# A fused linear-attention and gated-MLP kernel: one ordering rule between a ScalarE Exp and a TensorE sum, and a new hand-written order of all 1160 steps

## The chip, the cores and the metric

One core of one Trainium2 chip. The time is device microseconds of one execution of the whole kernel; the median of three runs is given, with the lowest and the highest.

## What is computed

The first half is a recurrent attention with a decay `alpha`, the second a gated MLP that mixes along the sequence. Batch 4, 8 heads, 768 steps, 48 columns per head, so rows of 8 x 48 = 384; the MLP has 1024 columns, half for `u` and half for `v`.

```
state = 0
for t in range(S):
    state = alpha[t][:, None] * state + outer(k[t], v[t])
    y[t] = q[t] @ state
x = y, heads side by side
h = relu(x @ w_in);  u, v = h[:, :512], h[:, 512:]
v_n = (v - mean(v)) / sqrt(var(v) + 1e-6)
v_s = w_spatial @ v_n + b_spatial        # along the sequence
out = (u * v_s) @ w_out
```

## The kernel before

The recurrence runs in chunks of 128 steps, 24 in all (i = 0 to 23), six to a batch. Chunks 0 to 7 are done two at a time, in pairs j = 0 to 3 (`pair`); chunks 8 to 23 one by one (`first`). The steps have short names, and the order is a list of these names:

- `ac kc qc vc`: loads of alpha, k, q and v (L436 for a pair, L646 for a chunk), all issued by SyncE's queue (SP).
- `lnp` takes the logarithm of alpha (ScalarE, L447). `cump j 0` and `cump j 1` (TensorE, L456) sum it along the steps, for the even and the odd rows, each into a bank of PSUM. `totp j` (TensorE, L473, 8 small matmuls) puts the totals of the pair into spare columns of the bank of the odd rows.
- `einvp j par` (ScalarE, L464) is the inverse Exp, exp(-x), of such a bank into `binvp`; `eexpp j par` (ScalarE, L485) is the forward Exp, in place in the bank. `ebcp j` (L559) is the Exp of the totals. `par` 0 is the first of the two, 1 the second.
- `ktp` and `qtp` (L490, L497) multiply k and q by these; `tr` (L518) transposes them; `ev` copies the transposes out of PSUM; `vbp` casts v.
- `updq` (L553) makes the pair's state updates, `z i` (L333, L335, VectorE) adds one to the state, `S i` (L340, VectorE or GpSimd) multiplies by the decay, `sb i` (L200, GpSimd, two casts) writes the state where TensorE reads it. These go from chunk to chunk, one after the other.
- `sc` (L583) makes the scores, `m` (L594) masks them, `ya` (L610) and `y i` (L623) make the output of a chunk from the scores and from the state of the chunk before.
- `xs`, `xt` and `xe` cast the output (L198 or L200), transpose it (L370 for pairs, L393 for single chunks) and copy it into `xT`.
- For single chunks the same steps are `cum` (L666, L669), `einv`, `eexp`, `trk` (L719), `upd` (L740), `sc` (L754), `y` (L776, L782).
- The MLP, for batch b: `v b c` and `u b f h` (three matmuls each with `w_in`, L828), `bn`, `rs`, `vn` (the normalization: L893/L894, L917/L918, then L925 on VectorE or L931 and L934 on GpSimd), `s` (six matmuls with the transposed spatial weights, in two halves, L828), `g` (L989), `o` (four matmuls with `w_out`, L828) and `st`, the store (L1046).

Every engine runs its own instructions in the order in which `replay` emits them. That order is `PLAN`, a table of 1160 words: a letter for the engine (P TensorE, D VectorE, A ScalarE, G GpSimd, S and Q a DMA's issue and its landing) and the number of the step. Numbers behind a P, as in `P119:448:128`, are columns of filler matmuls (`junk`, L188) that TensorE runs ahead of the step. Many steps may stand on one of two engines, and the table says which. The table comes from a search that is not part of the file; `replay` only asserts that each step stands behind the steps that it names in `got(...)`.

TensorE's matmuls differ in the part of the array that they use. L583 uses 48 rows by 64 columns, L553, L610, L393, L719 and L840 64 by 128, L754 48 by 128, L857 1 by 128; all others use 128 by 128.

Of the kernel before, what the change touches and what calls it, by code (L numbers as in the profile page):

```python
# [58 lines left out]
P119:448:128:64:192:192:384 P68 G63 S114 Q115 P58 A70 P69 P129 A59 S112 Q113 G72 P130 A80 A60 D61 A71 G74 A120 S180
Q181 D73 A121 P64:512 D6 A141 A131 P75:128 D62 A132 P77:128 S116 Q117 D123 A78 P66:128 D134 A76 P79 A67 D65 S184 Q185  # L60
G122 D81 P90 D82 P265 D84 A266 D92 G85 S182 Q183 A188 P87:64:192 D91 G133 P127 P125 A128 D88 P199 G8 P200 P138 A201
D89 P136 S19 Q20 G83 A202 A211 P189:192 D135 A139 G124 D126 A190 S186 Q187 G10 P140 A191 P93 D204 A137 D7 D142 P97 A94
S325 Q326 D143 P148 A98 D193 P95 G203 P208 D145 A96 P197 D149 P99 P151 G192 A100 D150 A198 P206 S24 Q25 A209 D153 A207
P195:64:64 A23 P267 G21 D22 P218 A196 G144 A268 D152 P101 D219 S329 Q330 G146 P104 A102 D220 A205 G194 P215 S327 Q328
P154 A105 D217 G86 P210 D216 G147 A333 P155 P159 D212 P221 D213 A156 D103 S29 Q30 P222 A160 G214 P344 S331 Q332 P157
P334 A346 D223 G27 P161 A158 P226 D106 P345 A162 G26 P163 A335 A347 D227 P174 A356 A164 D28 D349 P224 A336 S33 Q34
P168 D165 A225 S386 Q387 P228 P230 A229 D338 A175 G348 P233 A169 D176 A231 P353 G337 P342 S390 Q391 P351 A354 D232
P172 A107 P170 A234 G32 D343 P340 A352 D173 P166 A177 G31 D171 A341 P366 A167 D235 G108 P250 S37 Q38 P247 A350 A252
P243:64 S388 Q389 G178 D367 A248 A249 P239 A251 D368 G339 A35 S428 Q429 P241 G36 D240 P355 A394 D244 P253 G109 A236
D179 P395 P245 A254 S430 Q431 G237 A255 D357 A242 D358 P273 D238 A396 G359 P277 D360 A397 A246 D361 P274 A399 G362  # L70
P278 D400 D275 P256 S392 Q393 G40 P363 A258 A257 P281 D364 A39 P282 S41 Q42 G398 D279 P269 D365 S432 Q433 G280 P259
P262 D283 P402 A260 A263 P270 D264 G276 A261 D404 A403 P293 A436 D271 G284 P294 S499 Q500 P409 D295 P369 G401 D410
P373 P437 G272 D374 P405 A439 P297 A370 S465 Q466 D411 A438 P375 P371 P298 D376 S467 Q468 G440 A372 A441 P412 D299 A45
P377 S434 Q435 G296 A413 D442 P285 D406 A378 G44 P414 P444 A46 D379 G407 A416 P380 G408 S503 Q504 P286 D415 D446 A381
P420 D43 S501 Q502 D445 A473 P426 D287 A507 P301 D382 S471 Q472 A421 G288 A427 P451 P508 G443 S469 Q470 D453 P417 A509
G300 D452 A511 P447 S596 Q597 P474 A302 P424 D448 A475 D512 P309 S505 Q506 G510 A418 A425 P422 D419 A476 G480 A478
S598 Q599 P454 A310 G477 P289 A455 S630 Q631 D479 P290 A383 D449 P481 A423 D291 S600 Q601 P456 G450 P514 A457 D483
# [1096 lines left out]
```

## Time and profile before

| | |
|---|---|
| median of 3 runs | 141.24 us (140.65 to 141.47) |
| the profiled execution | 141.2 us, of which 139.4 us is the span from the first to the last instruction |
| busy, share of the span | TensorE 95%, VectorE 86%, GpSimd 71%, ScalarE 70% |
| granted TensorE clock | 0.996 |
| moved by DMA | 28.64 MB, mean 205 GB/s |

How to read it: a group of instructions shows the line, the engine, the operation, what it writes and reads, the shapes and the count, then the busy time, the mean duration in ns, and the idle time of the engine just before with what ended it. PE is TensorE's matmul, PEld its weight load, which runs beside matmuls; DVE is VectorE, ACT ScalarE, POOL GpSimd, SP SyncE. Matmuls overlap, so that TensorE's real pace is read from the start of one to the start of the next, and a busy PE may still be waiting a little. In the timeline the columns are the start, the time taken and the instructions; behind them, in brackets, the idle time ahead and its releaser.

### The profile page before, as it was taken

How to read it: one execution, taken by the hardware profiler on the slowest of the kernel's cores; microseconds unless marked ns; L12 is line 12 of the kernel's file. 1: busy time of each engine (PE TensorE's matmuls, PEld its weight loads, DVE VectorE, ACT ScalarE, POOL GpSimd, SP SyncE). 2: the span in 40 equal slices, each digit the busy share in tenths (PEclk: the TensorE clock that was granted, in tenths of full speed). 3: DMA queues.
4: the chain of work that ended last, by engine and by line, in shares of the span. 5: the costliest groups of instructions: out<-in, count | busy, mean ns of one | idle time of the engine just before them, and what ended most of it. 6: DMA issues, size and time to landing. Idle time of an engine off the chain costs nothing.

```text
span 139.4 us, 5013 instructions
## 1 busy us (share of the span) xinstructions
PE 133.0 (95%) x1931; PEld 85.0 (61%) x1931; DVE 120.3 (86%) x283; ACT 97.9 (70%) x278; POOL 99.1 (71%) x176
## 2 busy tenths in 40 slices
PE   6999789999999999999999999999999999999990
PEld 4677566756666656665666765655566665555660
DVE  7159899999998898888999999999798999987970
ACT  3597768899944979999975798898772776840011
POOL 6964996697899868697098899988779574382300
PEclk9999999999999999999999999999999999999998
DMA  4999999999989999799999989999981040007635
GB/s 108 324 323 325 289 326 334 312 240 319 282 190 281 182 217 218 151 232 173 197 211 190 232 165 197 203 214 259 291 164 42 0 163 16 0 3 286 224 143 196
DMA packets 89000, 28.64 MB, mean 205 GB/s; under 512 B 83728, under 2 KB 87440, under 8 KB 88976
## 3 DMA queue, kind: packets, MB, share of 16 engines
q1 hardware_dynamic: 88944, 28.32, 82.0%
q8 instruction: 15, 0.25, 0.7%
q14 instruction: 9, 0.07, 0.1%
q0 software_dynamic: 32, 0.00, 0.0%
HBM read 23.60 MB, written 4.72 MB: 203 GB/s over the span
## 4 chain that ended last, share of the span: by engine, by line
PE 78%; POOL 7%; SPq 4%; DMA 4%; DVE 2%; issue 2%; ACT 1%; ACTq 0%; POOLq 0%; DVEq 0%
PE bank L828 54%; SPq L436 4%; DMA kc<-in_k_dram 4%; PE bank L754 3%; PE bank L719 3%; POOL vn L934 2%; PE bank L782 2%; PE bank L740 2%; PE bank L666 2%; PE bank L776 2%; PE bank L393 1%; PE bank L518 1%; POOL sbd L200 1%; POOL kt L490 1%; PE bank L583 1%
## 5 line engine op out<-in xcount | busy, mean ns | idle before, releaser
L828 PE MATMUL bank<-w_spT,vn 128*128 128x384 bf16 x192 | 36.2, 326 | 0.1
L989 POOL TENSOR_TENSOR gT<-vsb,uT 128x384 bf16<-128x384 f32 x24 | 22.0, 928 | 5.6 <-DVE vsb L976 5.3
L828 PEld LDWEIGHTS <-vn 128*128 128x128 bf16 x192 | 17.3, 97 | 12.1 <-POOL vn L934 1.3
L765 DVE TENSOR_TENSOR ptm<-bank,mask 128x512 bf16<-128x512 f32 x32 | 20.6, 682 | 1.2 <-PE bank L754 1.0
L828 PE MATMUL bank<-xT,w_in 128*128 128x384 bf16 x96 | 19.7, 326 | 0.0
L976 DVE TENSOR_TENSOR vsb<-bank,bsp_bc 128x384 f32<-128x384 f32 x31 | 16.8, 553 | 3.1 <-PE bank L828 2.2
L828 PE MATMUL bank<-w_out_sb,gT 128*128 128x384 bf16 (+1 forms) x100 | 18.7, 319 | 0.0
L828 PE MATMUL bank<-w_in,xT 128*128 128x512 bf16 x72 | 18.7, 379 | 0.0
L690 POOL TENSOR_TENSOR kt<-kc,binv 128x384 bf16<-128x384 f32 x15 | 13.6, 913 | 6.5 <-ACT binv L678 6.3
L200 POOL CAST sbd<-state 64x192 bf16<-64x192 f32 x40 | 14.1, 352 | 5.5 <-DVE state L340 2.4
L934 POOL TENSOR_SCALAR vn<-v_sb,rstd,nb 128x512 bf16<-128x512 bf16 x17 | 13.6, 799 | 1.7
L893 DVE BATCH_NORM_STATS2 stats<-v_sb 128x6 f32<-128x512 bf16 x20 | 13.6, 681 | 0.8 <-ACT v_sb L208 0.8
L208 ACT ACTIVATE v_sb<-bank 128x512 bf16<-128x512 f32 x18 | 10.8, 599 | 3.6 <-PE bank L828 3.6
L208 ACT ACTIVATE uT<-bank 128x384 bf16<-128x384 f32 x18 | 8.8, 494 | 5.6 <-PE bank L828 5.5
L828 PEld LDWEIGHTS <-gT 128*128 128x128 bf16 x100 | 8.9, 97 | 5.4 <-DVE gT L989 0.2
L198 ACT COPY kqT<-bank 128x256 f32<-128x256 f32 x32 | 11.1, 381 | 1.1 <-PE bank L719 1.1
L828 PEld LDWEIGHTS <-w_in 128*128 128x128 bf16 x96 | 8.4, 98 | 5.2 <-DVE w_in L200 0.3
L188 PE MATMUL bank<-junk 128*128 128x64 f32 (+5 forms) x32 | 9.7, 433 | 1.1 <-DVE junk L1059 1.1
L594 DVE TENSOR_TENSOR ptm<-bank,mask 128x512 bf16<-128x512 f32 x16 | 10.1, 680 | 0.4 <-PE bank L583 0.2
L198 ACT CAST x_sb<-bank 128x384 bf16<-128x384 f32 x19 | 8.8, 481 | 2.1 <-PE bank L782 1.4
L700 DVE TENSOR_TENSOR qt<-qc,bank 128x384 bf16<-128x384 f32 x16 | 8.7, 549 | 1.1 <-ACT bank L695 1.0
L828 PEld LDWEIGHTS <-xT 128*128 128x128 bf16 x72 | 6.0, 97 | 5.1 <-ACT xT L198 0.2
(133 smaller groups left out, 297.8 us busy)
## 6 DMA issues: line engine op xcount, KB each, us to landing
ac<-in_alpha_dram SPq DMA_DIRECT2D x16, 192.0 KB, 3.9
qc<-in_q_dram SPq DMA_DIRECT2D x16, 192.0 KB, 3.8
kc<-in_k_dram SPq DMA_DIRECT2D x16, 192.0 KB, 3.9
vc<-in_v_dram SPq DMA_DIRECT2D x16, 192.0 KB, 3.8
raw_w<-in_moe_w_spatial_dram SPq DMA_DIRECT2D x3, 768.0 KB, 6.8
out_dram<-raw_w SPq DMA_DIRECT2D x11, 192.0 KB, 3.3
out_dram<-o_sb SPq DMA_DIRECT2D x9, 192.0 KB, 2.3
ac<-in_alpha_dram SPq DMA_DIRECT2D x4, 384.0 KB, 4.4
```

What stands on the lines that cost most here:

```text
L188: nc.tensor.matmul(out=flat[:, 0:cols].rearrange("p (a b) -> p a b", a=4), lhsT=junk, rhs=junk[:, None, 0:n].to_broadcast([128, 4, n]), st ...
L198: nc.scalar.copy(out=out, in_=in_)
L200: ENG[eng].tensor_copy(out=out, in_=in_)
L208: nc.scalar.activation(out=out, in_=in_, func=AF.Relu)
L594: nc.vector.tensor_tensor(out=st[f"ptm{par}"][:, s], in0=st[f"pt{s}{par}"], in1=mask2[:, par], op=ALU.mult)
L690: ENG[eng].tensor_mul(out=k_blocks(kt3)[:, :, :, 0:D], in0=quad(st["kc"]), in1=st["binv"])
L765: nc.vector.tensor_tensor(out=st["ptm"][:, s], in0=st[f"pt{s}"], in1=mask4, op=ALU.mult)
L828: return lambda ps: nc.tensor.matmul(out=out(ps), lhsT=lhsT(), rhs=rhs(), start=start, stop=stop)
L893: nc.vector.bn_stats(out=stats, in_=d["v_sb"][:, tt, :])
L934: nc.gpsimd.tensor_scalar(out=d["vn"][:, t, :], in0=d["v_sb"][:, t, :], scalar1=d["rstd"][:, t:t + 1], scalar2=nb, op0=ALU.mult, op1=ALU.add)
L976: nc.vector.tensor_tensor(out=hold["vs"], in0=ps[:, 0:TH], in1=bsp_bc[:, th, :], op=ALU.add)
L989: ENG[eng].tensor_tensor(out=bt[b]["gT"][:, dsl, cols], in0=hold["vs"], in1=bt[b]["uT"][:, dsl, cols], op=ALU.mult)
```

## The change

Three things. `totp j` is recorded behind `einvp j 1` and depends on it, where it depended on `cump j 1` alone. `eexpp j 1` depends on `totp j` as well as on `einvp j 1`. And the whole table is another one. Lines behind the edit move down by two (L828 becomes L830, and so on) and L485 becomes L486. No step is added or taken away, and no instruction's shape changes.

```
-                op(("totp", j), "PE", 0.2, tot, got(("cump", j, 1), ("c_half",)), prio=P + 2.5, use=[sl_c[1]])
-
             op(("einvp", j, par), "ACT", 0.38, einv, got(("cump", j, par), ("ktp", *divmod(2 * j + par - 3, 2))), prio=P + 3,
                use=[sl_c[par]])
 
+            if par == 1:
+                op(("totp", j), "PE", 0.2, tot, got(("einvp", j, 1), ("c_half",)), prio=P + 2.5, use=[sl_c[1]])
+
...
-            op(("eexpp", j, par), "ACT", 0.38, eexp, got(("einvp", j, par)), prio=P + 3.1, use=[sl_c[par]])
+            op(("eexpp", j, par), "ACT", 0.38, eexp,
+               got(("einvp", j, par), *((("totp", j),) if par else ())), prio=P + 3.1, use=[sl_c[par]])
```

The first line of the table, before and after:

```
-S110 Q111 D0 D15 D2 G16 D5 S49 Q50 D3 D4 D1 D13 G9 D11 S55 Q56 G47 Q48 D12 D17 G14 A118 S51 Q52 G18 A57 S53 Q54
+S110 Q111 D0 D17 D5 G47 Q48 D3 D6 D1 S49 Q50 D11 D2 D15 S53 Q54 D13 D12 G14 D4 A118 S51 Q52 G16 A57 S55 Q56
```

It also hands steps to other engines. Over the whole program VectorE has 15 of the 24 `vn` instead of 7, 3 of the 20 `S` instead of 10, and 7 of the 32 `u` copies instead of 14; GpSimd has 17 `S` instead of 10 and 9 `vn` instead of 17; ScalarE has 25 `u` copies instead of 18.

ScalarE at the start, before: the Exps of pairs 0 and 1 (`binvp` is the inverse, a bank onto itself the forward Exp, `bc` the Exp of the totals).

```order
L464 ACTIVATE binvp_114<-bank_86 128x384
L464 ACTIVATE binvp_113<-bank_87 128x384
L559 ACTIVATE bc_223<-bank_86 128x8
L485 ACTIVATE bank_87<-bank_87 128x384
L485 ACTIVATE bank_86<-bank_86 128x384
L464 ACTIVATE binvp_115<-bank_85 128x384
L485 ACTIVATE bank_85<-bank_85 128x384
L559 ACTIVATE bc_240<-bank_88 128x8
```

The same place now:

```order
L464 ACTIVATE binvp_113<-bank_86 128x384
L486 ACTIVATE bank_86<-bank_86 128x384
L464 ACTIVATE binvp_114<-bank_87 128x384
L464 ACTIVATE binvp_115<-bank_85 128x384
L486 ACTIVATE bank_87<-bank_87 128x384
L464 ACTIVATE binvp_113<-bank_88 128x384
L486 ACTIVATE bank_85<-bank_85 128x384
L561 ACTIVATE bc_246<-bank_87 128x8
```

The even rows of pair 0 (now bank 86) come first with both of their Exps, and between the two Exps of the odd rows (bank 87) stands an Exp of pair 1; the Exp of the totals moved from third to eighth.

GpSimd at the start, before: from pair 0's k product to the state of chunk 3 (`state<-state,bc` is `S`, `sbd<-state` is `sb`, `mask_118` is half of a pair's mask, `mask_96` the mask of single chunks).

```order
L490 TENSOR_TENSOR kt_111<-kc,binvp_114 128x4x2x48
L200 CAST vbp<-vc 128x384
L490 TENSOR_TENSOR kt_112<-kc,binvp_115 128x4x2x48
L340 TENSOR_TENSOR state<-state,bc_223 128x192
L490 TENSOR_TENSOR kt_112<-kc,binvp_113 128x4x2x48
L253 MEMSET ut_ones 128x128
L246 AFFINE_SELECT ut_ones<-ut_ones 128x128
L200 CAST sbd_119<-state 64x4x48 x2
L200 CAST vbp<-vc 128x384
```

The same place now:

```order
L492 TENSOR_TENSOR kt_111<-kc,binvp_114 128x4x2x48
L340 TENSOR_TENSOR state<-state,bc_246 128x192
L246 AFFINE_SELECT mask_118<-mask_118 64x512 x2
L492 TENSOR_TENSOR kt_112<-kc,binvp_113 128x4x2x48
L200 CAST vbp<-vc 128x384
L340 TENSOR_TENSOR state<-state,bc_246 128x192
L200 CAST sbd_119<-state 64x4x48 x2
L492 TENSOR_TENSOR kt_111<-kc,binvp_115 128x4x2x48
L492 TENSOR_TENSOR kt_111<-kc,binvp_114 128x4x2x48
L340 TENSOR_TENSOR state<-state,bc_301 128x192
```

All five `S` of chunks 0 to 4 stand on GpSimd now, where two did, and half a mask that stood ahead of the k product stands behind the first `S`; one k product of pair 1 went to VectorE.

TensorE in the middle of the third batch, before: the end of the transpose of chunk 18's output (L393) and what follows.

```order
L393 MATMUL bank_89<-ident,x_sb 128x64
L393 LDWEIGHTS x_sb
L393 MATMUL bank_85<-ident,x_sb 128x64
L828 LDWEIGHTS vn
L828 MATMUL bank_86<-w_spT,vn 128x384
L828 LDWEIGHTS vn
L828 MATMUL bank_86<-w_spT,vn 128x384
```

The same transpose now:

```order
L393 MATMUL bank_90<-ident,x_sb 128x64
L393 LDWEIGHTS x_sb
L393 MATMUL bank_85<-ident,x_sb 128x64
L721 LDWEIGHTS kt_112
L721 MATMUL bank_86<-ident,kt_112 128x64
L721 LDWEIGHTS kt_112
L721 MATMUL bank_87<-ident,kt_112 128x64
```

Behind the transpose, which uses 64 rows of the array, stood a matmul with all 128 rows; now the transposes of two chunks' k and q follow (L721), which use 64 rows as well.

More of the change, by code (lines that the diff above doesn't have):

```diff
@@ L57 @@
 PLAN = """
-S110 Q111 D0 D15 D2 G16 D5 S49 Q50 D3 D4 D1 D13 G9 D11 S55 Q56 G47 Q48 D12 D17 G14 A118 S51 Q52 G18 A57 S53 Q54
[L59 to L77, printed above, removed]
@@ new lines @@
+S598 Q599 G510 A310 D448 P454 A302 S600 Q601 A425 P422 D512 G288 A383 D455 P481 A423 P514 G449 D482 P456 A483 P305
+D457 G292 A515 D419 A516 P484 A458 S602 Q603 A306 P488 D485 P517 A604 D490 P459 G486 S667 Q668 A513 D519 G450 P605
+A460 P313 S669 Q670 D489 G487 A606 P317 D518 A607 A609 G608 S630 Q631 A314 P491 D461 P520 A492 S709 Q710 G611 P321
+D610 A521 G384 D318 P493 S632 Q633 P612 A495 D494 P522 A462 P615 D613 P496 D523 A614 D524 G464 A675 D322 P532 A497
+P525 S634 Q635 D533 A498 D385 P619 A526 D616 S713 Q714 P534 D463 A527 P536 D621 S671 Q672 A638 P538 D528 A717 P548
@@ L109 @@
+P1129 S323 Q324 D1127 G1120 S578 Q579 P1130 P1132 D1131 G1128 P1140 A1133 P1152 S1134 Q1135 D1141 P1144 A1153 S1142
+Q1143 P1136 A1145 S1154 Q1155 P1148 S1146 Q1147 D1137 P1156 S1138 Q1139 A1149 A1157 S1150 Q1151 S1158 Q1159
 """
```

74 lines of the change are left out of this document (43 added, 31 removed).

## The prediction

> **What bounds the kernel now.** I read the page first, then the busy times by stage, then the timeline of TensorE and of the three engines that feed it.
>
> ```profile
> PE 133.0 (95%) x1931; PEld 85.0 (61%) x1931; DVE 120.3 (86%) x283; ACT 97.9 (70%) x278; POOL 99.1 (71%) x176
> PE   6999789999999999999999999999999999999990
> PEclk9999999999999999999999999999999999999998
> ```
>
> TensorE is busy in every slice but the first and the last few, and at full clock in 39 of 40 slices. By stage (the columns are the stretch, its length, then the busy time of each engine; the borders are where the first single chunk begins and where the last chunk's output is transposed):
>
> ```profile
> 0.00:36.30 36.30, 33.31 (x580) 23.30 (x580) 29.71 (x77) 28.16 (x73) 27.55 (x57) 1.00 1.01 293
> 36.30:118.00 81.70, 81.56 (x1242) 51.16 (x1238) 74.99 (x173) 63.42 (x188) 65.32 (x110) 1.00 0.86 184
> 118.00:139.40 21.40, 18.09 (x120) 10.57 (x116) 15.56 (x35) 6.36 (x18) 6.27 (x10) 0.98 0.38 139
> ```
>
> In the middle TensorE has 81.56 of 81.70 us, VectorE 6.7 us left, the others more. So a gain in the middle can only come from TensorE's own order, and a loss from an engine that makes it wait. Busy does not say that it streams at its pace; for that I read starts in TensorE's timeline:
>
> ```profile
> 32.40 0.65 PE L828 MATMUL bank<-xT,w_in 128*128 128x384 bf16 x3
> 32.98 0.42 PE L583 MATMUL bank<-kqT 48*64 48x128 bf16 x16
> ...
> 90.43 0.65 PE L828 MATMUL bank<-xT,w_in 128*128 128x384 bf16 x3
> 91.01 0.40 PE L754 MATMUL bank<-kqT 48*128 48x128 bf16 x8
> ...
> 92.08 0.65 PE L828 MATMUL bank<-xT,w_in 128*128 128x384 bf16 x3
> 92.57 0.81 PE L828 MATMUL bank<-w_in,xT 128*128 128x512 bf16 x3
> 93.22 0.65 PE L828 MATMUL bank<-xT,w_in 128*128 128x384 bf16 x3
> ...
> 117.78 0.48 PE L393 MATMUL bank<-ident,x_sb 64*128 64x64 bf16 x12
> 118.19 0.66 PE L828 MATMUL bank<-xT,w_in 128*128 128x384 bf16 x3
> ```
>
> Three matmuls of 384 columns take 0.49 us to the next start when a 128*128 matmul follows (92.08 to 92.57). When a matmul with another part of the array follows (the two numbers ahead of the shape) they take 0.58 us: 32.40 to 32.98 and 90.43 to 91.01. So each change of the array's shape costs 0.09 to 0.10 us. From 26 us to the last matmul the trace has 52 such changes, the first and the last of them quoted; start to start less the columns at that pace, they sum to 5.1 us, 0.098 us each. All other waits of TensorE in that stretch sum to 1.3 us. Ahead of it TensorE does wait:
>
> ```profile
> 16.52 0.58 PE L553 MATMUL bank<-vbp,kt 64*128 64x48 bf16 x32 [0.86 <-POOL vbp L200]
> 19.13 0.40 PE L518 MATMUL bank<-ident,qt 128*128 128x128 bf16 x4 [0.51 <-DVE qt L497]
> 24.87 0.57 PE L610 MATMUL bank<-vbp,ptm 64*128 64x48 bf16 x32
> 26.54 0.33 PE L623 MATMUL bank<-sbd,kqT 128*128 128x96 bf16 x4
> ```
>
> These are `updq 1`, a `tr q`, `ya 2` and `y 5`. Up to `y 5` the pairs' chain through VectorE and GpSimd sets the pace, behind it TensorE's work.
>
> **The change part by part.** The sum is made against the profiled execution: 139.4 us of span and 1.8 us around it, 141.2, which is the median of the runs (141.24) within what they scatter.
>
> *The rule itself.* Nothing is added. The wait of `totp` for an inverse Exp was there for pair 0 and cost TensorE 0.25 us:
>
> ```profile
> 7.20 0.34 PE L473 MATMUL bank<-halves_of,la 128*128 128x2 bf16 x8 [0.25 <-ACT binvp L464]
> 27.34 0.51 ACT L485 ACTIVATE bank<-bank 128x384 f32<-128x384 f32 x1
> ```
>
> New is that `eexpp j 1` holds ScalarE until TensorE has reached `totp j`. For pairs 0 and 1 another Exp stands in between. For pair 3 `totp 3` stands behind `y 5` on TensorE, and behind `eexpp 3 1` on ScalarE stand the first `rs`, `ebcp 3`, the copy of `v 0 3` and the second Exps of pair 3. If `y 5` keeps its place near 26.5 us this is covered, since `eexpp 3 1` ran at 27.34 us before; every us that `y 5` is late beyond 27.3 is paid here as well. I take 0; the bounds are -0.25 (the wait quoted) and the lateness of `y 5`, which is in the third rival.
>
> *The head, to `y 5`.* Rows for the steps that change engines:
>
> ```profile
> L340 POOL TENSOR_TENSOR state<-state,bc 128x192 f32<-128x192 f32 x10 | 5.4, 540 | 3.0 <-DVE state L335 2.7
> L340 DVE TENSOR_TENSOR state<-state,bc 128x192 f32<-128x192 f32 x10 | 5.0, 498 | 0.2
> L200 DVE CAST w_in<-raw_w 128x512 bf16<-128x512 f32 x2 | 1.4, 690 | 0.0
> L490 DVE TENSOR_TENSOR kt<-kc,binvp 128x384 bf16<-128x384 f32 x1 | 0.6, 559 | 3.8 <-DMA kc<-in_k_dram 3.8
> L200 DVE COPY xT<-bank 128x384 bf16<-128x384 bf16 x1 | 0.3, 348 | 0.0
> L490 POOL TENSOR_TENSOR kt<-kc,binvp 128x384 bf16<-128x384 f32 x7 | 7.0, 1007 | 2.3 <-DMA kc<-in_k_dram 2.2
> L200 DVE CAST x_sb<-bank 128x384 bf16<-128x384 f32 x5 | 2.7, 544 | 0.1
> L335 DVE TENSOR_TENSOR state<-bank,state 128x192 f32<-128x192 f32 x16 | 5.6, 350 | 0.7 <-PE bank L553 0.3 <-issue 0.2
> ```
>
> The ends of the head on the two engines (VectorE's last masks of pair 2, GpSimd's `sb 4`), and from the chain of waits what a `cump` and a transpose of a pair's chunk take of TensorE:
>
> ```profile
> 7.88 0.56 DVE L490 TENSOR_TENSOR kt<-kc,binvp 128x384 bf16<-128x384 f32 x1 [3.79 <-DMA kc<-in_k_dram]
> 21.51 3.30 DVE L594 TENSOR_TENSOR ptm<-bank,mask 128x512 bf16<-128x512 f32 x5
> ...
> 25.63 0.74 POOL L200 CAST sbd<-state 64x192 bf16<-64x192 f32 x2 [2.08 <-DVE state L340]
> ...
> 25.72 0.32 PE bank L456 x2
> 26.05 0.17 PE bank L370 x3
> ```
>
> VectorE runs from the first k product at 7.88 to the last mask at 24.81 us, nearly without a pause. In the new order the same stretch has the same 12 masks, 6 q products and 4 `z`, but not two `S` (2 x 0.498) and a weight cast (0.690), and one k product (0.559) and one `xT` copy (0.348) more: 0.78 us less, so `ya 2` could come at 24.1 instead of 24.87. The first k product waits for the same fourth load. GpSimd gets three more `S` (3 x 0.540). Its chain now ends with `z 4` on VectorE, which stands behind a cast of 0.54 us, then `S 4` (0.54) and `sb 4` (0.74): 24.81 - 0.78 + 0.54 + 0.35 + 0.54 + 0.74 = 26.2 against the 26.37 at which `sb 4` ended. So `y 5` stays near 26.3 to 26.5. But by then the new order has done more on TensorE: `v 0 2` (three of 512 columns, 0.65 us from 92.57 to 93.22) and one transpose (0.17) have moved ahead of `y 5`, one `cump` (0.32) behind it, a gain of 0.5. With the 0.2 at `sb 4` that is 0.7; as no queue has been seen in this order, I take 0.4. Bounds: 0.8 gained (all that VectorE drops) and the loss of the third rival.
>
> *Changes of the array's shape.* Counted in the two programs' order, by the shapes that the trace gives each line, before has 72 changes and the new order 64. Behind `y 5`, where TensorE is never idle for long, it is 52 and 48, since transposes and scores stand side by side more often. 4 x 0.098 = 0.39 us. The four in the head lie in time in which TensorE waits. Bounds: 0 if a wait grows in the same places, 0.78 for all eight. [...]
>
> *Steps on other engines in the middle.* Between the first single chunk and the last transpose VectorE's steps, by their mean durations, grow by 0.84 us (`vn` from 4 to 9, `o` 4 to 7, `g` 2 to 4; `u` 8 to 5, `S` 7 to 3, `ev` 13 to 11, each by its mean), of which it had 6.7 us to spare; ScalarE's grow by 1.7, GpSimd's shrink by 7.1, mostly from `vn` and casts of v:
>
> ```profile
> L934 POOL TENSOR_SCALAR vn<-v_sb,rstd,nb 128x512 bf16<-128x512 bf16 x17 | 13.6, 799 | 1.7
> L931 POOL TENSOR_SCALAR nb<-mvs,rstd 128x1 f32<-128x1 f32 x17 | 4.6, 269 | 5.3 <-ACT rstd L918 5.0
> L925 DVE TENSOR_SCALAR vn<-v_sb,mvs,rstd 128x512 bf16<-128x512 bf16 x7 | 3.5, 512 | 0.1
> PEld L828 <- POOL vn L934: 1.3, 3, 0.5
> ```
>
> A `vn` takes 1.07 us on GpSimd in two steps and 0.51 on VectorE. TensorE's weight load waited three times for one on GpSimd, 1.3 us in sum. I take 0: a search that packs VectorE tighter can lose elsewhere what it wins here. Bounds: -0.6 (about half of the 1.3, since the load runs ahead of the matmul) and +0.84.
>
> *Fillers, queues, the tail.*
>
> ```profile
> L188 PE MATMUL bank<-junk 128*128 128x384 f32 x2 | 1.0, 597 | 0.0
> ...
> ac<-in_alpha_dram SPq DMA_DIRECT2D x16, 192.0 KB, 3.9
> ```
>
> Fillers grow from 2944 to 3200 columns, all but the last 64 ahead of the first `v`; the longest single one, 384 columns, takes 0.6 us and would cost that if its step were ready; I take 0. On SP one store (`st 1 4`) now stands ahead of 15 loads; it is issued nine steps after its copy, so it waits for no more than that copy, 0.5 us, while a load has 3.9 us to land and nothing in the middle waited for one. The end is the same in kind: `s`, then the last `o` back to back, two last copies on ScalarE. 0, with 0.2 either way.
>
> Sum: 139.4 - 0.4 - 0.39 = 138.6, and 1.8 around it: **140.4 us**.
>
> **The rivals.** *Only the array's shape counts.* GpSimd's chain, with no slack by the working above, holds `y 5` at 26.9 or later and the head's gain is gone: 141.2 - 0.4 = 140.8. For it speaks that every `S` is on GpSimd; against it, VectorE's 0.78 us.
>
> *The middle's waits go as well.* With `vn` on VectorE 0.6 us of TensorE's waits disappear on top of the forecast: 139.8. Against it: VectorE was 92% busy there.
>
> *Slower: the state chain in GpSimd's queue.* Each `S` moved to GpSimd waits behind what runs there, a k product of 1.007 us at most, 0.5 in the middle, takes 0.04 more, and the next `z` waits behind a running mask on VectorE, half of 0.66 (3.30 for five). That is 0.87 for each of three, 2.6 us on the chain `z`, `S`, `z`. TensorE can cover about 1 us of it with `v 0 2` and `v 0 3`; 1.6 are left, and 0.4 come back from the shapes: 142.4. It decides where `y 5` starts after about 28 us. For it: GpSimd's `S` waited 2.7 us for `z` already with fewer of them, 2.08 us stood ahead of `sb 4`. Against it: the chain has pauses in which VectorE works on masks that do not depend on it.
>
> **How the numbers follow.** The forecast has 0.40, only the shapes 0.25, the middle's waits 0.10, slower 0.25. The range leaves out the lower half of the third rival and the upper half of the slower one: 139.4 to 142.2. About 0.5%, 0.7 us, is what a measurement of this kernel can tell: faster is below 140.5, slower above 141.9. The forecast's own spread, 139.9 to 140.9, is faster in 0.29 and the same in 0.11; the shapes alone 0.03, 0.20 and 0.02 slower; the middle's waits 0.10 faster; the slower case 0.05 the same and 0.20 slower. Faster 0.42, same 0.36, slower 0.22.
>
> **What would show it.** Right: `ya 2` starts near 24.1 to 24.4 and `y 5` near 26.5 with `v 0 2` done; 48 changes of shape behind `y 5`, still 0.1 us each; TensorE's other waits behind it near 1.3 us. Wrong: `y 5` after 28 us with GpSimd's `S` and `sb` in the chain of waits (the slower rival), a wait of ScalarE for `totp 3` with the copy of `v 0 3` behind it, or TensorE waiting for VectorE between 60 and 90 us by more than 1 us.

## The result and the profile after

The new kernel takes 139.52 us, the median of four runs (139.07 to 139.96), against 141.24 us before: ratio 0.9881, 95% interval 0.9843 to 0.9919. It is 1.7 us faster where 0.8 was forecast, inside the range by 0.1 us. Medians here and below are of all runs; ratios and intervals leave out runs that took over 1.5% more than the fastest of their kernel (two of seven with the added 128-row matmuls, four of twelve without fillers, one of twelve with the engines of `vn` back, two of twenty-four of the kernel before). The profiled execution is the run of 139.07 us, with 137.3 us of span.

The busy times and two rows of slices of the new kernel's page:

```profile
PE 131.5 (96%) x1931; PEld 88.0 (64%) x1943; DVE 116.2 (85%) x278; ACT 101.1 (74%) x286; POOL 92.8 (68%) x165
PE   6999999999999999999999999999999999999990
PEclk9999999999999999999999999999999999999999
```

By stage, cut at the same two events as before (first single chunk begins, last output transposed):

```profile
0.00:36.20 36.20, 34.62 (x608) 26.36 (x611) 28.89 (x77) 28.95 (x74) 28.09 (x61) 1.00 0.99 294
36.20:116.14 79.94, 79.06 (x1212) 50.90 (x1214) 74.93 (x175) 63.95 (x190) 58.95 (x98) 1.00 0.86 178
116.14:137.30 21.16, 17.79 (x121) 10.72 (x121) 12.39 (x29) 8.24 (x24) 5.74 (x7) 1.00 0.49 179
```

The head is 0.1 us shorter, the middle 1.76, the tail about 0.24. The cut by events hides something: the new order has done more work by 36.2 us than the old one had by 36.3. So the head has gained more than 0.1, and it shows in the middle. Busy time of TensorE says little either way: it was over 98% of the middle before as now. (The trace holds 60 of the 72 records of 512 columns, so gaps of 0.2 us next to those aren't waits.)

TensorE's timeline at the end of the head; `ya 2`, `v 0 2`, a transpose, `y 5`, `totp 3`:

```profile
24.15 0.56 PE L612 MATMUL bank<-vbp,ptm 64*128 64x48 bf16 x30
...
25.69 0.59 PE L830 MATMUL bank<-w_in,xT 128*128 128x512 bf16 x2
26.13 0.33 PE L370 MATMUL bank<-ident_q,x_sb 128*128 128x128 bf16 x3
26.29 0.33 PE L625 MATMUL bank<-sbd,kqT 128*128 128x96 bf16 x4
26.46 0.34 PE L473 MATMUL bank<-halves_of,la 128*128 128x2 bf16 x8
```

`ya 2` starts at 24.15 us instead of 24.87, `y 5` at 26.29 instead of 26.54, now behind `v 0 2`. The two chains that lead there, VectorE's masks of pair 2 and GpSimd's `sb 4`:

```profile
20.19 3.69 DVE L596 TENSOR_TENSOR ptm<-bank,mask 128x512 bf16<-128x512 f32 x6
```

```profile
25.44 0.72 POOL L200 CAST sbd<-state 64x192 bf16<-64x192 f32 x2
```

The masks end at 23.88 us instead of 24.81, `sb 4` at 26.16 instead of 26.37. To split the rest, I take TensorE's time from its first matmul to its last apart: the columns of each useful matmul at the pace at which the same kind streams elsewhere, the fillers, 0.098 us for every change of the array's shape, and what is left, which is waiting. These sums are mine, from starts in TensorE's timeline; stretches end at the start of the event named. A change between 48 and 64 rows of 128 columns isn't counted: 11 such changes stand behind `y 5` before and 9 now, and the starts there show no gap (0.026 or 0.052 us to the next start, where the same matmuls ahead of 128 rows have 0.123 or 0.148).

| us | before | after |
|---|---|---|
| useful columns | 115.94 | 115.94 |
| fillers | 4.91 | 5.33 |
| changes of shape | 72, 7.06 | 64, 6.27 |
| waits up to `ya 2` | 5.34 | 4.58 |
| waits, `y 5` to the first single chunk | 0.29 | 0.00 |
| waits, on to the transpose of chunk 8 | -0.04 | 0.30 |
| waits, on to the transpose of chunk 17 | 0.33 | 0.33 |
| waits, on to the transpose of chunk 22 | 0.65 | -0.08 |
| waits, on to the end | 0.30 | -0.01 |
| sum | 134.78 | 132.66 |

Of the 2.12 us between the two profiled executions, 0.78 are shapes (0.39 of them behind `y 5`), 0.77 waits of the head, 0.99 waits behind `y 5`; fillers take 0.42 back.

One row of the table is not what its name says. It prices every filler at the full pace, but the fillers ahead of the first product stream at half of it for most of their time:

```profile
1.05 4.81 PE L188 MATMUL bank<-junk 128*128 128x192 f32 x16 [1.05 <-DVE junk L1061]
5.70 0.33 PE L456 MATMUL bank<-la,le_pair 128*128 128x384 bf16 x1
```

These 1344 columns take 4.65 us from start to start, and 2.24 at the table's price. (A filler is two matmuls in the trace; those of 192 columns take 0.320 us to the next start up to 5.06 us, the first one 0.482, and 0.163 from 5.37 on.) So 2.4 of the 4.58 us up to `ya 2` are a slow start and not waiting; before, with 1408 columns in the same 4.65 us, it is 2.3 of 5.34. The difference of the two kernels hardly moves. By TensorE's timeline the pace changes near 5.3 us in both, so the two profiled executions compare fairly.

The rows of the steps that moved most, before and now, are those of `vn`:

```profile
L936 POOL TENSOR_SCALAR vn<-v_sb,rstd,nb 128x512 bf16<-128x512 bf16 x9 | 6.9, 768 | 0.9
L927 DVE TENSOR_SCALAR vn<-v_sb,mvs,rstd 128x512 bf16<-128x512 bf16 x15 | 5.8, 416 | 1.8 <-ACT rstd L920 1.8
```

The 1.3 us in which TensorE's weight load waited for a `vn` on GpSimd are gone from its list of waits.

The theory, then: the table brings the gain, in three parts (the head, fewer changes of shape, no waits for `vn` behind the head), and the rule brings nothing. The rivals: the head alone, or the assignment of `vn` alone, or the rule itself does it.

### The profile page after: what moved, and what is told of

It is laid out like the page before. It is cut to its first block, busy times and chain, and to the rows that moved or that the text cites. A ratio compares the mean times of both kernels' runs of the same rounds, so it can differ in the third digit from the quotient of the medians.

```text
span 137.3 us, 5011 instructions
## 1 busy us (share of the span) xinstructions
PE 131.5 (96%) x1931; PEld 88.0 (64%) x1943; DVE 116.2 (85%) x278; ACT 101.1 (74%) x286; POOL 92.8 (68%) x165
## 4 chain that ended last, share of the span: by engine, by line
PE 91%; DMA 3%; ACT 2%; issue 1%; SPq 0%; ACTq 0%
PE bank L830 57%; PE bank L721 3%; PE bank L756 3%; DMA ac<-in_alpha_dram 3%; PE bank L188 3%; PE bank L520 3%; PE bank L784 2%; PE bank L668 2%; PE bank L742 2%; PE bank L585 2%; PE bank L778 2%; PE bank L393 2%; PE bank L555 2%; PE bank L612 1%; PE bank L456 1%
## 5 line engine op out<-in xcount | busy, mean ns | idle before, releaser
L830 PE MATMUL bank<-w_spT,vn 128*128 128x384 bf16 x192 | 35.1, 326 | 0.0
L991 POOL TENSOR_TENSOR gT<-vsb,uT 128x384 bf16<-128x384 f32 x25 | 23.1, 938 | 9.2 <-DVE vsb L978 8.6
L830 PEld LDWEIGHTS <-vn 128*128 128x128 bf16 x192 | 17.5, 97 | 10.5
L830 PE MATMUL bank<-xT,w_in 128*128 128x384 bf16 x96 | 19.4, 326 | 0.0
L830 PE MATMUL bank<-w_out_sb,gT 128*128 128x384 bf16 (+1 forms) x100 | 18.2, 319 | 0.0
L830 PE MATMUL bank<-w_in,xT 128*128 128x512 bf16 x60 | 17.2, 379 | 1.0 <-issue 0.5
L208 ACT ACTIVATE uT<-bank 128x384 bf16<-128x384 f32 x25 | 11.9, 495 | 5.5 <-PE bank L830 5.5
L198 ACT COPY kqT<-bank 128x256 f32<-128x256 f32 x35 | 11.8, 386 | 2.8 <-PE bank L721 1.9
L340 POOL TENSOR_TENSOR state<-state,bc 128x192 f32<-128x192 f32 x17 | 9.5, 556 | 5.4 <-DVE state L333 2.6
L830 PEld LDWEIGHTS <-w_in 128*128 128x128 bf16 x96 | 8.7, 97 | 6.1
L830 PEld LDWEIGHTS <-gT 128*128 128x128 bf16 x100 | 8.9, 97 | 5.4 <-POOL gT L991 0.4
L188 PE MATMUL bank<-junk 128*128 128x64 f32 (+5 forms) x44 | 11.1, 378 | 1.1 <-DVE junk L1061 1.1
L188 PEld LDWEIGHTS bank<-junk 128*128 128x128 f32 x44 | 8.5, 235 | 2.0 <-DVE junk L1061 1.1
L662 ACT ACTIVATE la<-ac 128x384 bf16<-128x384 f32 x16 | 8.5, 534 | 1.1 <-DMA ac<-in_alpha_dram 1.1
```

Source lines behind the costliest of these rows:

```text
L188: nc.tensor.matmul(out=flat[:, 0:cols].rearrange("p (a b) -> p a b", a=4), lhsT=junk, rhs=junk[:, None, 0:n].to_broadcast([128, 4, n]), st ...
L198: nc.scalar.copy(out=out, in_=in_)
L208: nc.scalar.activation(out=out, in_=in_, func=AF.Relu)
L340: ENG[eng].tensor_tensor(out=st["state"], in0=st["state"], in1=st["bc"][:, :, None].to_broadcast([128, HP, D]), op=ALU.mult)
L830: return lambda ps: nc.tensor.matmul(out=out(ps), lhsT=lhsT(), rhs=rhs(), start=start, stop=stop)
L991: ENG[eng].tensor_tensor(out=bt[b]["gT"][:, dsl, cols], in0=hold["vs"], in1=bt[b]["uT"][:, dsl, cols], op=ALU.mult)
```

## The experiments

Times are to be compared through the ratio to the kernel before, timed beside it on the same chip: 141.4 us beside the first four, 141.35 beside the others. Differences of two ratios have an interval too: against the new kernel's 0.9843 to 0.9919 it is some 0.6 us to either side.

**The head alone** (new table up to `y 5`, old one behind it).

```
-S331 Q332 G213 P222 A158 P344 A223 G214 P163 D162 A345 D106 G28 P224 P226 A164 P346 D225 G27 P334 A347 D227 P174 G26
+S331 Q332 G213 P222 A158 P344 A223 G214 P163 D162 A345 D106 G28 P224 P226 P334 G27 P346 G26 A335 A347 D227 P174 A356
...
```

> The new order up to y 5, and behind it the old order of all that is left. Three-part theory (head 0.7 us, 4 changes of the array's shape 0.4 us, other waits of TensorE behind y 5 0.9 us): only the head's part is here, 52 changes of shape behind y 5 as before, so 140.3 to 140.7 us, with y 5 at 26.3 and v 0 2 done by then. Rival, the head gives nothing and all of the gain is in the rest: 141.2. Rival, all of the gain comes from the head: 139.5.

Measured: 141.43 us, ratio 1.0007 (0.9987 to 1.0026). Where the gain went is in TensorE's timeline:

```profile
28.21 0.66 PE L831 MATMUL bank<-xT,w_in 128*128 128x384 bf16 x3 [0.20 <-POOL w_in L201]
...
29.45 1.47 PE L831 MATMUL bank<-w_in,xT 128*128 128x512 bf16 x6 [0.41 <-ACT xT L199]
```

`y 5` starts at 26.50 us with `v 0 2` done, much as in the new kernel, but between it and the first single chunk TensorE waits 1.05 us instead of 0.29 before and 0.00 in the new kernel. The old order behind `y 5` can't feed a TensorE that arrives early: the gain of the head is lost in the next 10 us.

**The rest alone** (old table up to `y 5`, new one behind it).

```
-P334 A346 D223 G27 P161 A158 P226 D106 P345 A162 G26 P163 A335 A347 D227 P174 A356 A164 D28 D349 P224 A336 S33 Q34
+P334 A346 D223 G27 P161 A158 P226 P163 D162 D106 G28 P224 A164 P345 D225 A347 D227 P174 G26 A107 D165 P228 A356 P230
...
```

> The complement: the old order up to y 5 and the new one behind it, 48 changes of shape behind y 5. Three-part theory: shapes 0.4 and waits 0.9, so 139.7 to 140.2 us, with TensorE's other waits behind y 5 at 0.6 us or less. Rival, the head is all: 141.2. If the parts simply add, this run's gain and that of the run with the new head sum to 1.7 us.

Measured: 140.39 us, ratio 0.9915 (0.9882 to 0.9948). It too pays at the seam:

```profile
27.20 0.59 PE L828 MATMUL bank<-w_in,xT 128*128 128x512 bf16 x2 [0.25 <-ACT xT L198]
...
48.78 0.33 PE L776 MATMUL bank<-sbd,kqT 128*128 128x96 bf16 x4 [0.37 <-POOL sbd L200]
```

From `y 5` to chunk 8's transpose it waits 1.29 us, the new kernel 0.30; from there to the end its waits and shapes are the new kernel's within 0.05 us. So the halves don't add: 0.0 and 0.85% alone, 1.2% together. What is missing is about the size of the waits at the seams (0.8 to 1.0 us each). The order has to be valued as one piece.

**The rule without the new table** (old table; only the few steps swapped that the two dependencies force).

```
-Q181 D73 A121 P64:512 D6 A141 P131 P75:128 D62 A132 P77:128 S116 Q117 D123 A78 P66:128 D134 A76 P79 A67 D65 S184 Q185
+D73 A121 P64:512 D6 A130 P131 A141 P75:128 D62 A132 P77:128 S116 Q117 D123 A78 P66:128 D134 A76 P79 A67 D65 S184 Q185
...
```

> The old table with the two new dependencies and only the swaps that they force: totp 1 behind the first transpose of pair 0 and its filler of 512 columns, totp 2 behind a transpose of pair 1, ebcp 1 behind einvp 1 1. Theory, the rule as such is worth nothing: 141.0 to 141.5 us. Rival, the rule is what makes it faster: 139.5. Rival, the rule costs, as ScalarE is held until TensorE reaches totp: up to 0.5 us slower, 141.7.

Measured: 141.89 us, ratio 1.0035 (1.0018 to 1.0052): half a microsecond slower.

```profile
6.62 0.65 PE L456 MATMUL bank<-la,le_pair 128*128 128x384 bf16 x3 [0.60 <-ACT la L447]
...
10.35 0.34 PE L473 MATMUL bank<-halves_of,la 128*128 128x2 bf16 x8 [0.75 <-ACT binvp L464]
```

The second row is the rule: `totp 1` waits 0.75 us for the inverse Exp that it now stands behind, and `updq 0` starts at 12.18 us instead of 10.81. Not all of the 1.37 us is the rule's: the 0.60 in the first row is a wait for the logarithm of alpha, and in this execution alpha's load lands 0.48 us later (L447 starts at 4.53 us instead of 4.05, in the other traces at 4.05 to 4.34). That leaves some 0.9 us at `updq 0`. The twelve runs, 141.69 to 142.35, are what the half microsecond rests on. Nothing of the gain is the rule's. With the new table the steps stand in the demanded order anyway.

**The engines of `vn` alone** (old table, each `vn` on the engine that the new table gives it).

```
-Q38 P247 A350 A252 P172 A107 P170 A234 G32 D343 P340 A352 D173 P166 A177 G31 D171 A341 P366 A167 D235 G108 P250 S37
+Q38 P247 A350 A252 P172 A107 P170 A234 G32 D343 P340 A352 D173 P166 A177 G31 D171 A341 P366 A167 D235 D108 P250 S37
...
-D179 P395 P245 A254 S430 Q431 G237 A255 D357 A242 D358 P273 D238 A396 G359 P277 D360 A397 A246 D361 P274 A399 G362
+G179 P395 P245 A254 S430 Q431 D237 A255 D357 A242 D358 P273 G238 A396 G359 P277 D360 A397 A246 D361 P274 A399 G362
```

> The old table with nothing changed but the engine of 12 of the 24 vn, as the new table has them (10 from GpSimd to VectorE, 2 the other way). Theory, TensorE's other waits were waits for vn on GpSimd: the waits near 95.5 and 123.6 us (0.28 and 0.18 us) go, 140.6 to 140.9 us. Rival, VectorE in the old order is too full to take them and gives the time back in later copies: 141.2 or slower, with new waits of TensorE for VectorE.

Measured: 142.51 us, ratio 1.0074 (1.0049 to 1.0100). It is 1.1 us slower than before. TensorE's waits behind `y 5`:

```profile
38.76 0.82 PE L828 MATMUL bank<-w_spT,vn 128*128 128x384 bf16 x4 [0.39 <-POOL vn L934]
...
64.66 0.40 PE L754 MATMUL bank<-kqT 48*128 48x128 bf16 x8 [0.23 <-DVE kqT L200]
```

A `vn` that is now late on GpSimd holds TensorE at 38.76, and at 64.66 a copy of kqT that stands behind the added `vn` on VectorE. Waits from there to the end sum to 2.3 us against 1.2. "The engine of `vn` alone does it" falls.

**The engines of `vn` back** (new table, each `vn` on the engine of the old table).

```
-G350 A341 P168 G339 D173 A352 A343 G179 A236 P247:64 S390 Q391 P250 A169 D248 P366 D108 A251 P241 A252 D367 S392 Q393
+G350 A341 P168 G339 D173 A352 A343 D179 A236 P247:64 S390 Q391 P250 A169 D248 P366 G108 A251 P241 A252 D367 S392 Q393
...
```

> The new table with the vn on the engines of the old one (17 on GpSimd). Theory, vn on GpSimd makes TensorE wait: 0.3 to 0.9 us slower, 139.8 to 140.4. Rival, the waits went because the table as a whole is tighter: 139.4 to 139.7.

Measured: 141.12 us, ratio 0.9983 (0.9958 to 1.0007), 1.4 us behind the new kernel's ratio, more than the expected 0.3 to 0.9. TensorE's weight loads wait for `vn` again, three times:

```profile
PEld L830 <- POOL vn L936: 1.6, 3, 0.8
```

The waits are 1.32 us between the first single chunk and chunk 8's transpose (0.30 in the new kernel), 0.45 up to chunk 20 (0.03) and 0.59 in the tail (-0.01). So in the new order, and only there, the new engines of `vn` are worth 1.4 us: order and engines were chosen for each other. The three waits for a `vn` stand at 95.84, 98.14 and 125.61 us, in the later stretches. In the first stretch TensorE waits for other things: 0.45 us at 48.01 for an Exp of ScalarE (what made that late isn't shown), and 0.47 us for a copy of VectorE. For the copy, two rows of TensorE, two of VectorE, one of GpSimd:

```profile
36.38 0.24 PE L671 MATMUL bank<-ones_col,la 128*128 128x1 bf16 x4
37.09 2.12 PE L830 MATMUL bank<-w_spT,vn 128*128 128x384 bf16 x12 [0.47 <-DVE w_spT L200]
```

```profile
33.70 0.41 DVE L927 TENSOR_SCALAR vn<-v_sb,mvs,rstd 128x512 bf16<-128x512 bf16 x1
...
35.91 0.86 DVE L927 TENSOR_SCALAR vn<-v_sb,mvs,rstd 128x512 bf16<-128x512 bf16 x1
```

```profile
35.86 0.77 POOL L936 TENSOR_SCALAR vn<-v_sb,rstd,nb 128x512 bf16<-128x512 bf16 x1
```

The second `vn` of VectorE starts 0.05 us behind one of GpSimd and takes 0.86 us instead of the 0.41 of the one before; the copy of w_spT behind it comes late (in the new kernel it starts at 36.02, ahead of VectorE's next `vn`), and TensorE waits 0.47 us.

**The price of a change of shape.** In the new kernel every one of the 32 groups of `s` gets one more matmul of 16 columns, into columns that nobody reads. In one kernel it uses 64 rows of the array (two changes more in each group, 64 in all), in the other 128 (none).

```
             mms.append(mm(
...
+        mms.insert(2, mm(
+            lambda ps: ps[:, TH:TH + 16], lambda: ident[0:64, :], lambda: ident[0:64, 0:16], False, False))
```

The second kernel has `ident[0:128, :]` and `ident[0:128, 0:16]`.

> The new kernel with one more matmul of 16 columns in each of the 32 s groups, behind the second of its six, that uses 64 rows of the array; it writes columns of the bank that nobody reads. Theory, a change of the array's shape costs TensorE 0.098 us wherever TensorE is the bound: 64 changes more, 6.3 us, and about 0.03 us for each small matmul, 1 us: 146.3 to 147.3 us. Rival, the gap at a change is time that TensorE would lose anyway in a full pipeline: under 142.

> The same 32 small matmuls with all 128 rows, so that the array's shape doesn't change. Theory: 0.03 us each, 1 us in sum: 140.2 to 141 us. If it comes as slow as the one with 64 rows, it is not the change of shape that costs.

Measured: 146.83 us, ratio 1.0388 (1.0366 to 1.0409), and 140.91 us, ratio 0.9944 (0.9908 to 0.9979). By the ratios the difference is 6.3 us, 0.098 for each of the 64 (0.089 to 0.107 by the intervals). The profiled execution of the second took 141.96 us; its `y 5` starts at 27.89, so that it lost its time in the head. From `y 5` to the last matmul, the two traces differ by 6.1 us, 0.096 for each. The timeline of one group shows it, with 64 rows:

```profile
49.01 0.48 PE L830 MATMUL bank<-w_spT,vn 128*128 128x384 bf16 x2
49.43 0.18 PE L830 MATMUL bank<-ident 64*128 64x16 bf16 x1
49.54 0.82 PE L830 MATMUL bank<-w_spT,vn 128*128 128x384 bf16 x4
```

and with 128:

```profile
48.93 0.48 PE L830 MATMUL bank<-w_spT,vn 128*128 128x384 bf16 x2
49.25 0.17 PE L830 MATMUL bank<-ident 128*128 128x16 bf16 x1
49.28 0.81 PE L830 MATMUL bank<-w_spT,vn 128*128 128x384 bf16 x4
```

Into the group 0.42 us against 0.32, out of it 0.11 against 0.03: about 0.09 on either side.

**No fillers** (the new kernel without any of the matmuls on junk).

```
-P119:192:64:128:192:320:192:192:64 G9 P58 S114 Q115 G8 A59 P68:64 A60 D61 S112 Q113 A69 P129:256 D62 A120 P70 G72 A71
+P119 G9 P58 S114 Q115 G8 A59 P68 A60 D61 S112 Q113 A69 P129 D62 A120 P70 G72 A71
...
```

> The new kernel without any filler matmul. Prediction's view, fillers run where TensorE waits and cost nothing: 139.5 us. Rival, they hold up steps that were ready (the one of 256 columns stands ahead of totp 2, for which ScalarE waited 0.73 us): 139.0 to 139.3. Rival, without them TensorE's clock is lower in the first microseconds and the head gets longer: granted clock below 0.99 in the first 25 us, 140 or more.

Measured: 141.35 us, ratio 0.9969 (0.9941 to 0.9997), scattered from 140.0 to 142.8. The fillers are worth about 1.2 us by the intervals' middles. The first products of pairs 0 and 1:

```profile
5.13 0.48 PE L456 MATMUL bank<-la,le_pair 128*128 128x384 bf16 x1 [5.13 <-ACT la L447]
...
6.64 0.52 PE L456 MATMUL bank<-la,lt_pair 128*128 128x384 bf16 x1
6.96 1.48 PE L456 MATMUL bank<-la,le_pair 128*128 128x384 bf16 x4
...
12.44 1.06 PE L520 MATMUL bank<-ident,qt 128*128 128x128 bf16 x8
...
15.79 0.65 PE L456 MATMUL bank<-la,le_pair 128*128 128x384 bf16 x3 [0.32 <-ACT la L447]
```

From 6.64 to 6.96 us 384 columns take 0.32 us, and eight transposes of 128 take 1.06 at 12.44, where the new kernel's eight take 0.61. At 15.79 three times 384 end after 0.65 us, the pace of 0.16 that the new kernel has from its first useful matmul. So TensorE runs at half pace here, and still does in the four transposes at 13.86 us (0.107 us from start to start); in the scores behind them the pace doubles near 14.7 us. All the while the page's row of the granted clock shows full speed, from the first slice on:

```profile
PEclk9999999999999999999999999999999999999999
```

Without fillers the change to full pace took 9.6 us from the first matmul at 5.13, with pauses in between. Fillers don't remove the slow start. They move it ahead of the useful work: back to back from 1.05 us, TensorE reaches full pace near 5.3 us in the new kernel, near 4.2 in the one with the added 128-row matmuls (the two matmuls of its filler of 320 columns take 0.671 us in the mean, in the new kernel 0.741) and near 6.6 in the one with fillers at the start only, and the last two have the same fillers there as the new one. That is 3.2 to 5.6 us from the first filler. The first useful product waits for the fillers: in the new kernel it starts at 5.70 us, without them at 5.13.

`y 5` starts at 28.71 us, and the waits up to chunk 8 grow as well; behind that the kernel waits where the new one does.

**Fillers at the start only.**

```
-P119:192:64:128:192:320:192:192:64 G9 P58 S114 Q115 G8 A59 P68:64 A60 D61 S112 Q113 A69 P129:256 D62 A120 P70 G72 A71
+P119:192:64:128:192:320:192:192:64 G9 P58 S114 Q115 G8 A59 P68 A60 D61 S112 Q113 A69 P129 D62 A120 P70 G72 A71
...
```

> The new kernel with only the eight groups of fillers ahead of the first cump; the others (some 2.7 us of TensorE's time up to the third pair's masks) are left out. Theory: what the kernel without any filler lost is the slow start of TensorE (its first cumps of 384 columns came 0.33 us apart there, 0.165 us here), and the fillers ahead of the first cump alone buy that; the later ones fill time in which TensorE would wait. Then the cumps behind 5.7 us stay 0.165 us apart and the time is within 0.3 us of the new kernel's, 139.5 us (ratio to the kernel before 0.986 to 0.990). Rival: the later gaps bring the slow pace back; then groups behind a gap in the first 20 us show about twice their duration, and the time is 140.5 to 141.3 us (ratio 0.994 to 1.0). Second rival: the later fillers stand in the way of work; then it is faster than 139.2 us.

Measured: 140.20 us (139.25 to 140.65), ratio 0.9904 (0.9877 to 0.9930). In TensorE's timeline the first product still runs at half pace (0.32 us for 384 columns, from 6.01 to 6.33), against the expectation; from 6.64 us the full pace holds, through gaps of 0.8 us:

```profile
6.97 0.81 PE L456 MATMUL bank<-la,le_pair 128*128 128x384 bf16 x4
8.61 0.34 PE L473 MATMUL bank<-halves_of,la 128*128 128x2 bf16 x8 [0.83 <-ACT binvp L464]
9.04 0.40 PE L520 MATMUL bank<-ident,qt 128*128 128x128 bf16 x4
```

So the start's fillers buy most of what fillers buy, by the middles of the intervals. Whether the later ones buy anything stays open: the interval holds both the new kernel's 0.988 and a loss of half a per cent, and the profiled execution is the fastest of the six, so that it can't show where the others lost time. Three of those have a mean granted clock of 0.971 to 0.975, where the profiled one has 0.996. Whether that is the loss is open: of the runs without fillers the one at 0.975 is the second fastest.

**`S` back to VectorE** (chunks 0, 2 and 4, as in the kernel before).

```
-A141 D81 D122 P138:128 G82 P77 A139 P265 D78 A76 S184 Q185 G18 A266 D84 P125:128 A128 P87 A126 P90 D88 A188 P148 G133
+A141 D81 D122 P138:128 D82 P77 A139 P265 D78 A76 S184 Q185 G18 A266 D84 P125:128 A128 P87 A126 P90 D88 A188 P148 G133
...
-S331 Q332 G213 P222 A158 P344 A223 G214 P163 D162 A345 D106 G28 P224 P226 A164 P346 D225 G27 P334 A347 D227 P174 G26
+S331 Q332 D213 P222 A158 P344 A223 G214 P163 D162 A345 D106 G28 P224 P226 A164 P346 D225 G27 P334 A347 D227 P174 G26
```

> The new kernel with the S of pairs' chunks 0, 2 and 4 on VectorE, as in the kernel before, at the same places of the order. Theory: VectorE sets the pace up to ya 2 (it pauses 0.26 us between 13.6 and 24.4 us), so three more steps of about 0.4 us there put ya 2 and y 5 1.0 to 1.3 us later, and GpSimd's S cost nothing in the new order: 140.5 to 140.8 us, ratio 0.994 to 0.997. Rival, the slower case of the prediction in part: GpSimd's queue holds the state chain, S on it costs time though the sum came out faster; then ya 2 and y 5 come no later and the time is at or under 139.5 us (ratio 0.988 or lower).

Measured: 140.36 us, ratio 0.9936 (0.9915 to 0.9957). `ya 2` starts at 24.87 us, `y 5` at 27.50, 1.2 us later than in the new kernel. VectorE, then GpSimd:

```profile
11.74 1.31 DVE L492 TENSOR_TENSOR kt<-kc,binvp 128x384 bf16<-128x384 f32 x1
...
26.24 0.33 DVE L340 TENSOR_TENSOR state<-state,bc 128x192 f32<-128x192 f32 x1
```

```profile
11.72 0.92 POOL L492 TENSOR_TENSOR kt<-kc,binvp 128x384 bf16<-128x384 f32 x1 [1.02 <-DMA kc<-in_k_dram]
...
26.72 0.72 POOL L200 CAST sbd<-state 64x192 bf16<-64x192 f32 x2 [1.32 <-DVE state L340]
```

`S 4` stands behind `stats` in VectorE's queue until 26.24, and GpSimd waits 1.32 us for it: the rival of the prediction that was to make the kernel slower, with the engines exchanged. In the new kernel nothing waits for `S 4`. Part of the delay is the first row: VectorE's k product takes 1.31 us, where in the new kernel it takes 0.55.

**Two cuts in the fillers.** One kernel drops three groups ahead of the first scores, the other the one group ahead of the transposes behind which `totp 2` stands. (That is pair 2, counted from 0, which the expectation calls the second.)

```
-S180 Q181 A130 P66:384 D73 A121 P64:64 D63 P131 A80 A74 S116 Q117 D123 A132 P79:64 A65 D134 A67 P127 S182 Q183 P75
-A141 D81 D122 P138:128 G82 P77 A139 P265 D78 A76 S184 Q185 G18 A266 D84 P125:128 A128 P87 A126 P90 D88 A188 P148 G133
+S180 Q181 A130 P66:384 D73 A121 P64:64 D63 P131 A80 A74 S116 Q117 D123 A132 P79 A65 D134 A67 P127 S182 Q183 P75
+A141 D81 D122 P138 G82 P77 A139 P265 D78 A76 S184 Q185 G18 A266 D84 P125 A128 P87 A126 P90 D88 A188 P148 G133
```

```
-D92 S19 Q20 P199:64:128 A124 D89 P189 G135 A200 G85 D91 S186 Q187 P136:256 G83 P201 D149 P140 A202 G203 D150 A211 S325
+D92 S19 Q20 P199:64:128 A124 D89 P189 G135 A200 G85 D91 S186 Q187 P136 G83 P201 D149 P140 A202 G203 D150 A211 S325
```

> The new kernel without three groups of fillers (64, 128 and 128 columns, 0.9 us of TensorE's time between 10.1 and 12.9 us), which stand ahead of the first scores that VectorE's masks wait for (0.49 us, at 13.64 us). Theory: they only fill time in which TensorE waits for copies of kqT and the like; the masks begin at 13.6 us as before and the time stays at 139.5 us within 0.2 (ratio 0.986 to 0.989). Rival: they hold the scores; then the masks begin up to 0.49 us earlier, y 5 follows, and the time is 139.0 to 139.2 us. Second rival: without them the pace of TensorE drops (groups at twice their duration), and the time is over 140.2 us.

> The new kernel without the one group of fillers (256 columns, 0.43 us from 15.35 us) ahead of the transposes behind which the totals of the second pair stand; ScalarE's Exp of that pair waits 0.73 us for them, the one wait that the new rule has put into the trace. Theory (the rule itself costs nothing): the totals come 0.4 us earlier and that wait shrinks to 0.3 us, but VectorE, which reads the Exp's result at 17.6 us, comes to it without a pause from its own queue, so ya 2 and the time stay: 139.5 us within 0.2 (ratio 0.986 to 0.989). Rival: the wait is on the path; then ya 2 comes 0.3 to 0.4 us earlier and the time is 139.1 us (ratio 0.983 to 0.985).

Measured: 139.22 us, ratio 0.9861 (0.9833 to 0.9888), and 138.96 us, ratio 0.9840 (0.9821 to 0.9858). In the first kernel the masks start a little earlier, as VectorE's timeline shows:

```profile
13.38 3.68 DVE L596 TENSOR_TENSOR ptm<-bank,mask 128x512 bf16<-128x512 f32 x6 [0.46 <-PE bank L585]
```

13.38 against 13.64, but `y 5` stands at 26.37 against 26.29. What the fillers give back at the masks is lost before `y 5`. The second shortens the wait that the rule has brought; ScalarE in the new kernel, then there:

```profile
16.44 0.47 ACT L486 ACTIVATE bank<-bank 128x384 f32<-128x384 f32 x1 [0.73 <-PE bank L473]
```

```profile
16.55 0.47 ACT L486 ACTIVATE bank<-bank 128x384 f32<-128x384 f32 x1 [0.49 <-PE bank L473]
```

In its profiled execution (139.67 us, the slowest of its four) this brings nothing to `y 5`, which starts 13.39 us behind the first scores, in the new kernel 13.10. The first scores themselves come 0.35 us later there, since the slow start lasts beyond the fillers: the first product runs at half pace, from 6.01 to 6.33 us. The other three runs took 138.85 to 138.96; that their start was quicker isn't shown. Both are faster than the kernel before. Whether either beats the new kernel isn't settled: their intervals overlap with 0.9843 to 0.9919, and they weren't timed beside it.

## Why the prediction came out as it did

*The rule, taken as 0.* Nothing in the new kernel speaks against it, though no run has the new table without the rule. Under the old table it costs half a microsecond (0.25 to 0.74 by the interval). Its one new wait in the new trace is the 0.73 us above, at pair 2, which the prediction hadn't named; it looked at pair 3, where ScalarE doesn't wait at all. The Exp's result is read by VectorE, which comes to it from its own queue without a pause:

```profile
17.24 0.35 DVE L335 TENSOR_TENSOR state<-bank,state 128x192 f32<-128x192 f32 x1
17.61 1.13 DVE L499 TENSOR_TENSOR qt<-qc,bank 128x384 bf16<-128x384 f32 x2
```

*The head, worked out at 0.7, taken as 0.4.* The working was right, the discount wrong. The match is closer than the working deserves: the masks end at 23.88 us, 0.15 before the sum's 24.03, and `ya 2` starts 0.27 behind them, behind a state update on TensorE, where it started 0.06 behind them before. `ya 2` was to come at 24.1 and came at 24.15; `sb 4` was to end at 26.2 and ended at 26.16; `v 0 2` and the transpose stand ahead of `y 5`, the `cump` behind. `y 5` comes 0.25 us earlier with 0.49 us more of useful work done, 0.74 in sum. The kernel with `S` back on VectorE shows that no queue ate it: there `y 5` waits for VectorE's queue, in the new kernel for none.

*Changes of shape, 4 behind `y 5` at 0.098 us.* Right: 48 behind `y 5`, 64 in all, and 0.096 to 0.098 us for each of 64 added ones. The four of the head can't be told from its waits, so whether any of them is paid there, as in the bound of 0.78 for all eight, isn't shown.

*Steps in the middle, taken as 0, bounds -0.6 to +0.84.* This is the step that failed. TensorE's waits behind `y 5` went from 1.53 to 0.54 us, 0.99 less, beyond the bound. "About half of the 1.3, since the load runs ahead of the matmul" was too little (in the trace before, a load of `xT` starts at 92.41 us and its matmul at 92.57), and "a search that packs VectorE tighter can lose elsewhere" was true only of an order not made for it: with the old table the new engines of `vn` cost 1.1 us, with the new one the old engines cost 1.4. Neither sign could be read from sums of busy time. The sum itself was off as well: VectorE's steps in the middle were to grow by 0.84 us, and its busy time there went from 74.99 to 74.93; its `vn` took 0.416 us in the new kernel and not the 0.512 that the sum used. The rival "the middle's waits go as well" was given 0.10; with the head's full 0.7 it is what happened. The errors in the head and here lay on the same side, and that they ended 0.1 us inside the range is luck.

*Fillers at 0.* They grew by 0.42 us of TensorE's time, in time in which it would have waited. Nothing shows that they cost; the two cuts can't tell a gain from none. But those ahead of the first product end in either kernel at 5.70 us, 0.57 later than that product started without them; whether this costs anything wasn't tried. The 0.6 us read for the longest filler was the mean of one of its two halves, partly at half pace; in the new kernel the whole takes 0.73 us to the next start (8.49 to 9.22).

*The slower rival.* It didn't come. `y 5` isn't late, GpSimd's `S` and `sb` aren't in the way, and the mechanism itself showed up only when `S` was put back on VectorE.

Sum of the terms as measured, against the profiled execution before: 0.74 for the head, 0.39 for the shapes behind it, 0.99 for the waits behind it, 2.12 us, where 0.4, 0.39 and 0 were forecast. The medians differ by 1.72, since the profiled execution after was the fastest of its four.

## What to carry to other kernels

Where a searched order replaces another, value it stretch by stretch on the engine that sets the pace (columns, changes of shape, waits), and trust a chain that you have added up step by step: here the added-up head came out to within 0.05 us (some of it by luck), and the discount on it was the error. Don't price an engine assignment apart from the order that it was chosen with; the same swap of `vn` was worth a gain of 1.4 us in one order and a loss of 1.1 in the other. A part of a new order, tried alone, can lose at its seam what it gains inside, as the head did here, so a part that gives nothing alone isn't shown to be worth nothing. (The order comes from a search; the title calls it hand-written.)
